# First product of the second network as seven products of half blocks instead of eight (Strassen's method), in a fused attention and two-network kernel on one core

## The chip, the cores and the metric

The kernel runs on one core of one Trainium2 chip, in one launch. The metric is device time in microseconds. Five engines run their own instruction queues in order and meet only at semaphores: TensorE (PE in the profile), VectorE (DVE), ScalarE (ACT), GpSimd (POOL) and SyncE (SP), which here only issues DMAs. TensorE multiplies out of the on-chip memory SBUF and accumulates in the eight banks of PSUM.

## The reference

Three stages follow each other. The change lies in the last one, `_moe2_ref`.

```python
def _moe2_ref(x, w_in, w_out):          # x 1536 x 512, w_in 512 x 2048, w_out 2048 x 512
    h = x @ w_in
    g = np.where(h > 0.0, h, 1.0 * (np.exp(np.minimum(h, 0.0)) - 1.0))
    return (g @ w_out).astype(np.float32)

def reference(**kwargs):
    attn_out = _attn_ref(...)           # 2 x 8 heads x 768 x 64: windowed and summary keys
    x = attn_out ... reshape(B * S, H * D)
    x = _moe_ref(x=x, ...)              # RMS norm, (silu(x @ w_gate) * (x @ w_val)) @ w_out, inner width 1536
    return _moe2_ref(x=x, ...)
```

The inputs arrive as 64-bit numbers. The kernel turns the weights into 32-bit numbers on the chip.

## The kernel before, in words

The 1536 tokens are cut into three blocks of 512 (`NBLK`, `TB`). Activations lie with features on the 128 partitions and tokens in the free dimension. `add_block1` runs the first network for a block in 12 chunks of 128 inner features, `add_block2` the second in 16. Attention for later blocks is woven into the first network of the earlier ones. By the end of the first network nothing but `add_block2` is left, three blocks one after another.

**Every large product is three matmuls.** A 32-bit number is split into a rounded high part and the rest, both of type `fp32r`. `THREE` in `project` (L894) and `down` (L960) multiplies high by high, high by rest and rest by high. The high part is an ACT cast (`split_a`, `act_a`, `x_hi`, all through `copy`, L300), the rest a subtraction (`split_b`, `act_b` through `minus` at L313, `x_lo` at L884).

**A chunk of `add_block2`** (L1015): `add_split` splits 512 columns of `w_in` (`ws_i`) and of `w_out` (`ws_p`); `add_project` makes 12 matmuls of 512 tokens into one PSUM bank (`ph`, L899: four parts of the contraction, three matmuls each); `elu_a` takes the exponential on ACT out of the bank (L939); `elu_b` on DVE makes min(exp, 1) - 1 (L943), `elu_c` on DVE adds max(ph, 0), again out of the bank (L947); `act_a` and `act_b` split the result; `down` adds 12 matmuls into the four banks `acc` (L967). So a block is 16 x 12 matmuls `ph` and as many `acc`, and the three blocks are 576 of each.

**Weights** arrive in `fetch`, and `convert_a` to `convert_d` (L424 to L448) make 32-bit numbers of them: an ACT pass, then on DVE a shift (L437 for w_in and w_out of this network), an insertion of the sign (`convert_c`, L442, left out for the kinds in `SIGNED`) and the lowest bits (L448). The 32-bit weights stay in the pool `raw` (36 tiles), for use by all three blocks.

**The order of the work** on each engine is made by `Order.issue` (L79) when the program is built. Each step is recorded by `add` with its engine, a cost, a due time, what it reads and writes, and the pool tiles that it takes (L60). The planner starts, per engine, the due step that can run; `SHIFT` moves due times by kind of step and by stretch; `SHARED` (L29) lists steps that it doesn't put on DVE and POOL at the same moment. The result is a fixed sequence per engine; the chip then goes through it by semaphores. Pools that matter here: PSUM banks `m0`, `m1`, `t0`, `t1` for `ph` (four), `a0` to `a3` for `acc`; `ws` (4 tiles of split weights), `act` (2 tiles of split activations), `x` (1), `raw` (36), `t2` (4).

Of the kernel before, what the change touches and what calls it, by code (L numbers as in the profile page):

```python
# [29 lines left out]
    "add_square", "diagonal", "x_lo", "x_hi", "act_a", "act_b", "elu_b", "convert_a", "convert_b", "convert_c",  # L30
# [186 lines left out]
def fused_kernel(ctx: ExitStack, tc: tile.TileContext, q, k, v, w_gate, w_val, w_out, rms_g, w_in2, w_out2, out):  # L217
# [16 lines left out]
    C2 = DFF2 // P  # L234
    TB = 512
# [24 lines left out]
    pool("ws", 4, True)  # L260
    pool("x", 1, True)
# [616 lines left out]
    def x_hi(eng, src, dst, c, i):  # L878
        t = new("x", dst, [P, 2, KM, TB], F32R) if dst not in T else T[dst]
        copy(eng, t[:, 0, c, i], T[src][:, c, i])  # L880

    def x_lo(src, dst, c, i):
        t = T[dst]
        nc.vector.tensor_sub(t[:, 1, c, i], T[src][:, c, i], t[:, 0, c, i].bitcast(F32))  # L884

# [363 lines left out]
```

## Time and profile before

| | us |
|---|---|
| median of 3 runs | 646.75 (645.97 to 647.37) |
| span of the profiled execution, first to last instruction | 644.8 |
| median less span | 1.95 |
| PE busy | 630.3 (98%) |
| DVE busy | 454.8 (71%) |
| ACT busy | 342.4 (53%) |
| POOL busy | 95.6 (15%) |

The page is one profiled execution. Its busy shares are means over the span; a stretch of it is read with the view by windows. The duration of one instruction is longer than its share of a dense sequence, since an engine begins the next before the last has left it: where instructions stand close together, the distance from start to start is the price. The page gives the profiled execution's span, and no time around it; the sum in the prediction is made on the span, and 1.95 us are added to compare with the median.

### The profile page before, as it was taken

The page shows a single profiled execution, that of the slowest core. Times are in us where ns is not written, and L with a number is a line of the kernel's source. Part 1 is how long each engine was busy: PE and PEld are TensorE (multiplying, and loading weights), DVE is VectorE, ACT ScalarE, POOL GpSimd, SP SyncE. Part 2 cuts the span into 40 slices and gives each one's busy share as a digit, 9 for nine tenths or more (in the row PEclk, how much of TensorE's full clock was granted, in tenths as well). Part 3 has the DMA queues.
Part 4 walks back from the last instruction along what each step waited for, and adds up shares of the span by engine and source line. Part 5 has one row for each costly group of instructions (what it writes and reads, how often), then busy time and mean ns, then how long its engine had stood idle before and what let it go on. Part 6 is the DMA issues. An engine that isn't in the chain of part 4 may idle for free.

```text
span 644.8 us, 9843 instructions
## 1 busy us (share of the span) xinstructions
PE 630.3 (98%) x3644; PEld 516.3 (80%) x3644; DVE 454.8 (71%) x828; ACT 342.4 (53%) x739; POOL 95.6 (15%) x160
## 2 busy tenths in 40 slices
PE   7899999999999999999999999999999999999997
PEld 5678777788888888888888888888888888888885
DVE  4788878868964557499999975555765555855554
ACT  2797568975463633465555564434444444544442
POOL 5753356363210210000000000000000000000000
PEclk9999999999999999999999999999999999999999
DMA  9998858565500000025656300000010000100001
GB/s 217 243 225 211 213 156 237 179 137 176 162 1 0 2 1 0 2 67 180 185 166 207 110 1 1 1 1 1 1 65 1 1 1 1 65 1 1 2 0 66
DMA packets 80352, 52.94 MB, mean 82 GB/s; under 512 B 51504, under 2 KB 75312, under 8 KB 80304
## 3 DMA queue, kind: packets, MB, share of 16 engines
q1 hardware_dynamic: 80304, 52.31, 29.9%
q8 instruction: 29, 0.48, 0.3%
q14 instruction: 19, 0.16, 0.1%
HBM read 49.15 MB, written 3.15 MB: 81 GB/s over the span
## 4 chain that ended last, share of the span: by engine, by line
PE 84%; DVE 6%; DMA 3%; SPq 3%; ACT 2%; issue 1%; DVEq 0%; ACTq 0%
PE acc L967 34%; PE ph L899 20%; PE pg L899 13%; PE pv L728 1%; PE pv_7c L899 1%; PE pv_8c L899 1%; PE pv_9c L899 1%; PE pv_11c L899 1%; PE pv_10c L899 1%; PE s L676 1%; PE pv_4c L899 1%; DMA va<-in_v 1%; DMA st_o<-in_moe_w_out 1%; PE pv_6c L899 1%; PE pv_1c L899 1%
## 5 line engine op out<-in xcount | busy, mean ns | idle before, releaser
L899 PE MATMUL ph<-xb,ws_i 128*128 128x512 f32 x576 | 137.9, 389 | 0.0
L967 PE MATMUL acc<-ws_p,act 128*128 128x512 f32 x576 | 137.7, 389 | 0.0
L967 PEld LDWEIGHTS acc<-ws_p,act 128*128 128x128 f32 x576 | 108.1, 188 | 22.5
L899 PEld LDWEIGHTS ph<-xb,ws_i 128*128 128x128 f32 x576 | 108.1, 188 | 22.4
L899 PE MATMUL pg<-x,ws_g 128*128 128x512 f32 (+1 forms) x456 | 108.7, 383 | 1.6 <-DVE ws_g L313 0.9
L967 PE MATMUL acc<-act,ws_o 128*128 128x512 f32 x432 | 106.3, 392 | 0.0
L899 PEld LDWEIGHTS pg<-x,ws_g 128*128 128x128 f32 x456 | 81.5, 188 | 19.1 <-DVE ws_g L313 1.3
L967 PEld LDWEIGHTS acc<-act,ws_o 128*128 128x128 f32 x432 | 80.4, 188 | 17.1 <-issue 0.5
L939 ACT ACTIVATE ex<-ph 128x512 f32<-128x512 f32 x48 | 28.8, 599 | 105.0 <-PE ph L899 105.0
L943 DVE TENSOR_SCALAR ex<-ex 128x512 f32<-128x512 f32 x48 | 20.5, 427 | 87.5 <-ACT ex L939 87.5
L302 ACT CAST act<-ex 128x512 fp32r<-128x512 f32 x48 | 29.8, 620 | 21.6 <-DVE ex L947 21.6
L302 ACT CAST ws_v<-raw_v 128x512 fp32r<-128x512 f32 x36 | 22.3, 620 | 32.6 <-PE acc L967 9.7
L932 DVE SCALAR_TENSOR_TENSOR th<-th,pg 128x512 f32<-128x512 f32 x36 | 24.6, 684 | 20.5 <-ACT th L928 20.3
L313 DVE TENSOR_TENSOR ws_i<-raw_i,ws_i 128x512 fp32r<-128x512 f32 x48 | 33.1, 689 | 8.0 <-ACT ws_i L302 8.0
L302 ACT CAST ws_i<-raw_i 128x512 fp32r<-128x512 f32 x48 | 29.7, 620 | 12.1 <-PE acc L967 12.1
L928 ACT ACTIVATE th<-pg 128x512 f32<-128x512 f32 x36 | 21.4, 595 | 26.7 <-PE pg L899 26.6
L313 DVE TENSOR_TENSOR act<-ex,act 128x512 fp32r<-128x512 f32 x48 | 33.1, 689 | 3.2 <-ACT act L302 0.7
L947 DVE SCALAR_TENSOR_TENSOR ex<-ph,ex 128x512 f32<-128x512 f32 x48 | 33.2, 691 | 1.5
L313 DVE TENSOR_TENSOR ws_p<-raw_p,ws_p 128x512 fp32r<-128x512 f32 x48 | 32.8, 682 | 1.2 <-ACT ws_p L302 1.2
L302 ACT CAST ws_p<-raw_p 128x512 fp32r<-128x512 f32 x48 | 29.6, 616 | 6.7 <-PE acc L967 6.7
L313 DVE TENSOR_TENSOR ws_o<-raw_o,ws_o 128x512 fp32r<-128x512 f32 x36 | 27.7, 770 | 6.3 <-ACT ws_o L302 6.2
L302 ACT CAST ws_o<-raw_o 128x512 fp32r<-128x512 f32 x36 | 22.3, 620 | 16.1 <-PE acc L967 3.5
(214 smaller groups left out, 918.8 us busy)
## 6 DMA issues: line engine op xcount, KB each, us to landing
st_i<-in_moe_w_in SPq DMA_DIRECT2D x16, 512.0 KB, 3.9
st_p<-in_moe_w_out SPq DMA_DIRECT2D x16, 512.0 KB, 3.8
st_g<-in_moe_w_gate SPq DMA_DIRECT2D x12, 512.0 KB, 4.9
st_o<-in_moe_w_out SPq DMA_DIRECT2D x12, 512.0 KB, 5.5
st_v<-in_moe_w_val SPq DMA_DIRECT2D x12, 512.0 KB, 4.9
va<-in_v SPq DMA_DIRECT2D x20, 192.0 KB, 5.6
kr<-in_k SPq DMA_DIRECT2D x12, 256.0 KB, 5.0
out<-ob SPq DMA_DIRECT2D x11, 256.0 KB, 2.0
```

Source lines behind the costliest of these rows:

```text
L302: nc.scalar.copy(out=out, in_=in_)
L313: (nc.gpsimd if eng == POOL else nc.vector).tensor_sub(out, a, b)
L676: nc.tensor.matmul(pq[h][ts, pr, :], qb[hs, pr, ts], ka[n][hs, pr, :], start=not pre, stop=not pre or pr == NP - 1)
L728: nc.tensor.matmul(pv[64 * h:64 * h + 64, pr, n, :], va[:NK, 2 * pr + h, :], T[f"ats{b}_{j}_{h}"][:, pr, QT * n:QT * n + QT], start=True, ...
L899: nc.tensor.matmul(pt[:, i], wt[:, a, kk * P:(kk + 1) * P], xt[:, c, kk, i], start=(kk == 0 and n == 0), stop=(kk == KM - 1 and n == 2))
L928: nc.scalar.activation(out=new("t2", f"th{b}_{c}", [P, TB]), in_=T[f"pg{b}_{c}"], func=AF.Tanh, scale=0.5)
L932: nc.vector.scalar_tensor_tensor(th, th, 1.0, T[f"pg{b}_{c}"], op0=ALU.add, op1=ALU.mult)
L939: nc.scalar.activation(out=new("t2", f"ex{b}_{c}", [P, TB]), in_=T[f"ph{b}_{c}"], func=AF.Exp)
L943: nc.vector.tensor_scalar(ex, ex, 1.0, -1.0, op0=ALU.min, op1=ALU.add)
L947: nc.vector.scalar_tensor_tensor(ex, T[f"ph{b}_{c}"], 0.0, ex, op0=ALU.max, op1=ALU.add)
L967: nc.tensor.matmul(acc, lhsT, rhs, start=(first and n == 0), stop=(last and n == 2))
```

## The change

The 512 x 512 part of w_in that four chunks share, and the 512 x 512 activations of a block, are each seen as two by two blocks of 256 x 256. The Winograd form of Strassen's method makes the four result blocks from seven products in place of eight.

- Per block of tokens: four sums of quarters of the activations (`x_sum`), and seven split factors (`factor_a`, `factor_b`).
- Per group of four chunks (`u`, four in a block): four sums of quarters of the weights on POOL (`w_sum`), seven splits of weights (`wide_a` on ACT, `wide_b` on DVE), seven products, each in one of the four PSUM banks.
- `save` (ACT, one a group) and `combine` (DVE, seven a group) add the products up, a bank and an SBUF tile each time.
- The ELU reads the sums in SBUF: `elu_a` makes max(-c, 0) on ACT, `elu_b` exp of its negative on ACT, `elu_c` on DVE the larger of that less 1 and of c.
- `down2` makes the same 576 matmuls as `down`, each step for 256 tokens and 256 inner features.
- w_in is fetched in 256 x 256 quarters, `i` and `p` join `SIGNED` (no `convert_c` for them), the activations `x` of the first network are four tiles for one, `ws` has 6 tiles for 4, `LEN_2` is 5.3 for 5.65, and the whole table `SHIFT` is new.

```diff
-    pool("ws", 4, True)
-    pool("x", 1, True)
+    pool("ws", WS, True)
+    pool("x", 4, True)
+    PAIRS = ("11", "21", "t2", "t1", "22", "t3", "t4")
+    FACTORS = ("i0", "i1", "s2", "s1", "s4", "s3", "i3")
+    def w_sum(eng, b, u, dst):
+        a11, a12, a21, a22 = [T[f"raw_i{4 * u + n}"].bitcast(F32) for n in range(4)]
+        t = new("raw", f"w{b}_{u}_{dst}", [P, TB])
...
+        (e.tensor_sub if minus_ else e.tensor_add)(t, x, y)
+    def wide_a(eng, b, u, i):
+        copy(eng, new("ws", f"ws{b}_{u}_{i}", [P, 2, 512], F32R)[:, 0], T[weight_of(b, u, i)].bitcast(F32))
+    def wide_b(eng, b, u, i):
+        t = T[f"ws{b}_{u}_{i}"]
+        minus(eng, t[:, 1], T[weight_of(b, u, i)].bitcast(F32), t[:, 0].bitcast(F32))
+    def product(b, u, i, bank, tag):
+        pt = new(tag, bank, [P, TB])
+        wt, xt = T[f"ws{b}_{u}_{i}"], T[f"xq{b}_{i}"]
+        for m in range(2):
+            for kk in range(2):
+                for n, (a, c) in enumerate(THREE):
+                    nc.tensor.matmul(
+                        pt[:, m * HALF:(m + 1) * HALF], wt[:, a, kk * HALF + m * P:kk * HALF + (m + 1) * P], xt[:, c, kk],
+                        start=kk == n == 0, stop=kk == 1 and n == 2)
+    def combine(src, other, dst):
+        nc.vector.tensor_add(new(TMP, dst, [P, TB]), T[src], T[other])
-    def elu_a(b, c):
-        nc.scalar.activation(out=new("t2", f"ex{b}_{c}", [P, TB]), in_=T[f"ph{b}_{c}"], func=AF.Exp)
...
-        nc.vector.tensor_scalar(ex, ex, 1.0, -1.0, op0=ALU.min, op1=ALU.add)
...
-        nc.vector.scalar_tensor_tensor(ex, T[f"ph{b}_{c}"], 0.0, ex, op0=ALU.max, op1=ALU.add)
+    def elu_a(src, ex):
+        nc.scalar.activation(out=new("t2", ex, [P, TB]), in_=T[src], func=AF.Relu, scale=-1.0)
+    def elu_b(ex):
+        nc.scalar.activation(out=T[ex], in_=T[ex], func=AF.Exp, scale=-1.0)
+    def elu_c(src, ex):
+        nc.vector.scalar_tensor_tensor(T[ex], T[ex], -1.0, T[src], op0=ALU.add, op1=ALU.max)
...
-            add_project(f"ph{n}", MM + AT, f"ws{b}_i{c}", x, [0], t)
+            for dst, at in (("s1", 0), ("s2", 1.5), ("s4", 3.5), ("s3", 5.0)):
+                add(SUM_W, 0, t - 6 + at, w_sum, b, u, dst, r=need[dst], w=[f"w{n}_{dst}"], new=[("raw", f"w{n}_{dst}")])
+            plus(1, "h1", "c00")
+            plus(2, "h1", "h2")
+            plus(3, "h2", "h4")
+            plus(4, "h4", "c01")
+            plus(5, "h4", "c11")
+            plus(5, "h2", "h3")
+            plus(6, "h3", "c10")
-SIGNED = 'gvo'
+SIGNED = 'gvoip'
-LEN_A, LEN_1, LEN_2 = 8.875, 7.05, 5.65
+LEN_A, LEN_1, LEN_2 = 8.875, 7.05, 5.3
```

How the order moves, at the places that the prediction speaks of. **PE before**, in the first block of the second network (`ph` is the first product, `acc` the second; names are those of tiles, with the buffer's number last):

```order
L899 MATMUL ph_7_4544<-xb_4242,ws_i_4528 128x512 x12
L967 MATMUL acc_0_2_4366<-ws_p_4462,act_0_5_4503 128x512 x3
L967 MATMUL acc_0_3_4370<-ws_p_4462,act_0_5_4503 128x512 x3
L967 MATMUL acc_0_0_4336<-ws_p_4500,act_0_6_4541 128x512 x3
L967 MATMUL acc_0_1_4340<-ws_p_4500,act_0_6_4541 128x512 x3
L899 MATMUL ph_8_4582<-xb_4242,ws_i_4566 128x512 x12
```

**PE now**, at the end of the third and through the fourth group of the first block (`p` are products, their numbers the block and the group; `xq` the factor of the activations, `ws` that of the weights):

```order
L1075 MATMUL p_0_2_4922<-xq_6_3742,ws_2_6_4871 128x256 x12
L1075 MATMUL p_0_3_4941<-xq_0_4241,ws_3_0_4875 128x256 x12
L1075 MATMUL p_0_3_4962<-xq_1_4997,ws_3_1_4892 128x256 x12
L1075 MATMUL p_0_3_4984<-xq_2_4252,ws_3_2_4912 128x256 x12
L1075 MATMUL p_0_3_5005<-xq_3_4256,ws_3_3_4954 128x256 x12
L1075 MATMUL p_0_3_5030<-xq_4_2819,ws_3_4_4982 128x256 x12
L1075 MATMUL p_0_3_5048<-xq_5_3704,ws_3_5_4999 128x256 x12
L1075 MATMUL p_0_3_5072<-xq_6_3742,ws_3_6_5024 128x256 x12
L1094 MATMUL acc_0_2_4481<-ws_p_4748,act_0_201_4916 128x512 x3
```

Before, each group of 12 `ph` stood between as many `acc`; now products can stand up to eight in a row, of half as many columns each, and the second product follows later.

**DVE now**, at the same place (L1083 is `combine`, which reads a bank `p`; L315 is a subtraction, with `wide_b` where it writes `ws`; L957 is `elu_c`):

```order
L1083 TENSOR_TENSOR c_0_2_4956<-p_0_2_4922,h_0_2_4937 128x512
L957 SCALAR_TENSOR_TENSOR ex_211_4935<-ex_211_4935,c_0_2_4918 128x512
L315 TENSOR_TENSOR ws_3_3_4954<-w_3_s_4794,ws_3_3_4954 128x512
L306 CAST xq_0_4977<-x_1_3558 128x512
L315 TENSOR_TENSOR ws_3_4_4982<-w_3_s_4854,ws_3_4_4982 128x512
L957 SCALAR_TENSOR_TENSOR ex_210_4959<-ex_210_4959,c_0_2_4956 128x512
L1083 TENSOR_TENSOR c_0_3_5022<-p_0_3_4962,h_0_3_5002 128x512
L1083 TENSOR_TENSOR h_0_3_5026<-p_0_3_4984,h_0_3_5002 128x512
L315 TENSOR_TENSOR ws_3_5_4999<-w_3_s_4873,ws_3_5_4999 128x512
L315 TENSOR_TENSOR ws_3_6_5024<-raw_i_4629,ws_3_6_5024 128x512
```

DVE had one subtraction per 512 columns of w_in and one ELU step out of the bank at this place; now `combine` is the one kind of step that reads a bank, and the others read two tiles of SBUF.

**POOL now**, over the same place (before, POOL has no step in the second network):

```order
L1035 TENSOR_TENSOR w_3_s_4873<-raw_i_4197,raw_i_4585 128x512
L1035 TENSOR_TENSOR w_0_s_4920<-raw_i_3470,raw_i_3524 128x512
L1035 TENSOR_TENSOR w_0_s_4980<-w_0_s_4920,raw_i_3367 128x512
L1035 TENSOR_TENSOR w_0_s_5020<-raw_i_3421,w_0_s_4980 128x512
L1035 TENSOR_TENSOR w_0_s_5063<-raw_i_3367,raw_i_3470 128x512
```

The 48 sums of weights are the whole of POOL's work from here on: the tile `w_3_s_4873` is for the fourth group, the `w_0` behind it for the first group of the next block.

## Rows read from the trace of the kernel before

**Rows 1.** The page: span, busy time of PE, and 40 slices of the span

```profile
span 644.8 us, 9843 instructions
...
PE   7899999999999999999999999999999999999997
...
DVE  4788878868964557499999975555765555855554
...
PEclk9999999999999999999999999999999999999999
```

**Rows 2.** By windows: start:end, length, then busy us (instructions) of PE, PEld, DVE, ACT, POOL, clock, DMA

```profile
0.00:15.00 15.00, 11.64 (x77) 7.67 (x81) 6.25 (x17) 4.22 (x6) 9.13 (x47) 1.00 1.07 218
...
260.00:375.00 115.00, 115.00 (x509) 95.22 (x508) 107.42 (x191) 66.56 (x113) 0.00 (x0) 1.00 0.41 128
375.00:461.00 86.00, 86.00 (x381) 71.19 (x381) 47.81 (x80) 36.39 (x65) 0.00 (x0) 1.00 0.00 1
```

**Rows 3.** The chain that ended last: start, length, what (in us)

```profile
375.45 2.72 PE ph L899 x12
378.17 2.72 PE acc L967 x12
...
632.49 8.17 PE acc L967 x36
```

**Rows 4.** Timeline of PE, 46 to 68: start, length from first start to last end

```profile
54.35 1.60 PE L899 MATMUL pv_0c<-x,ws_v 128*128 128x256 f32 x12
55.79 1.60 PE L899 MATMUL pg<-x,ws_g 128*128 128x256 f32 x12
```

**Rows 5.** Groups by line and form: count, busy us, mean ns of one, idle before them

```profile
L899 PE MATMUL ph<-xb,ws_i 128*128 128x512 f32 x576 | 137.9, 389 | 0.0
...
L947 DVE SCALAR_TENSOR_TENSOR ex<-ph,ex 128x512 f32<-128x512 f32 x48 | 33.2, 691 | 1.5
L313 DVE TENSOR_TENSOR act<-ex,act 128x512 fp32r<-128x512 f32 x48 | 33.1, 689 | 3.2 <-ACT act L302 0.7
...
L302 ACT CAST act<-ex 128x512 fp32r<-128x512 f32 x48 | 29.8, 620 | 21.6 <-DVE ex L947 21.6
...
L939 ACT ACTIVATE ex<-ph 128x512 f32<-128x512 f32 x48 | 28.8, 599 | 105.0 <-PE ph L899 105.0
...
L943 DVE TENSOR_SCALAR ex<-ex 128x512 f32<-128x512 f32 x48 | 20.5, 427 | 87.5 <-ACT ex L939 87.5
...
L448 DVE SCALAR_TENSOR_TENSOR raw_i<-st_i,raw_i 128x512 uint16<-128x512 uint16 x16 | 12.0, 750 | 0.0
...
L442 DVE SCALAR_TENSOR_TENSOR raw_i<-st_i,raw_i 128x512 uint32<-128x512 uint32 x16 | 11.0, 689 | 0.0
...
L437 DVE TENSOR_SCALAR raw_i<-st_i 128x512 uint32<-128x512 uint32 x16 | 6.8, 422 | 0.0
```

**Rows 6.** Timeline of DVE, 379 to 382

```profile
379.91 0.68 DVE L313 TENSOR_TENSOR ws_i<-raw_i,ws_i 128x512 fp32r<-128x512 f32 x1
380.51 0.68 DVE L313 TENSOR_TENSOR ws_p<-raw_p,ws_p 128x512 fp32r<-128x512 f32 x1
```

**Rows 7.** Timeline of POOL, 131 to 134

```profile
131.22 1.29 POOL L799 TENSOR_TENSOR slice(0, 512, None)_2057<-slice(0, 512, None)_2057,slice(0, 512, None)_2067 128x512 f32<-128x512 f32 x1
132.52 1.27 POOL L313 TENSOR_TENSOR ws_g<-raw_g,ws_g 128x512 fp32r<-128x512 f32 x1
133.75 1.30 POOL L799 TENSOR_TENSOR slice(0, 512, None)_2057<-slice(0, 512, None)_2057,slice(0, 512, None)_2080 128x512 f32<-128x512 f32 x1
```

**Rows 8.** Timeline of POOL, 57 to 58 and 71 to 73

```profile
57.30 1.29 POOL L313 TENSOR_TENSOR ws_v<-raw_v,ws_v 128x512 fp32r<-128x512 f32 x1 [0.28 <-ACT ws_v L302]
...
71.93 1.29 POOL L313 TENSOR_TENSOR ws_v<-raw_v,ws_v 128x512 fp32r<-128x512 f32 x1 [6.36 <-ACT ws_v L302]
```

**Rows 9.** Timeline of DVE, 57 to 59 and 71 to 75

```profile
57.75 0.69 DVE L932 SCALAR_TENSOR_TENSOR th<-th,pg 128x512 f32<-128x512 f32 x1 [2.31 <-ACT th L928]
...
72.34 1.42 DVE L313 TENSOR_TENSOR ws_o<-raw_o,ws_o 128x512 fp32r<-128x512 f32 x1 [1.26 <-ACT ws_o L302]
```

More of the change, by code (lines that the diff above doesn't have):

```diff
@@ L29 @@
 SHARED = (
-    "add_square", "diagonal", "x_lo", "x_hi", "act_a", "act_b", "elu_b", "convert_a", "convert_b", "convert_c",
+    "add_square", "diagonal", "x_lo", "x_hi", "act_a", "act_b", "elu_c", "x_sum", "w_sum", "factor_a", "factor_b",
+    "wide_b", "convert_a", "convert_b", "convert_c",
     "convert_d", "split_a", "split_b", "copy_keys", "normalize")
@@ L234, in fused_kernel @@
     C2 = DFF2 // P
+    U2 = C2 // 4
     TB = 512
@@ L317, in fused_kernel @@
     ANY_SB = {ACT: 0.52}
+    SUM_X = {DVE: 0.6}
+    SUM_W = {POOL: 1.28}
+    TMP = ("e", "ats")
     masks = [const.tile([P, NK], F32, name=f"mask{var}") for var in range(3)]
@@ new lines, in save, with down2 @@
+    def save(eng, src, dst):
+        copy(eng, new(TMP, dst, [P, TB]), T[src])
+    def combine(src, other, dst):
+        nc.vector.tensor_add(new(TMP, dst, [P, TB]), T[src], T[other])
+    def down2(b, u, m, n, first, last, qs=(0, 1)):
+        ot = T[f"act2_{b}_{u}{m}{n}"]
+        for j in range(2):
+            wt = T[f"ws{b}_p{4 * u + 2 * m + j}"]
+            for q in qs:
+                name = f"acc2_{b}_{2 * n + q}"
+                acc = new(f"a{2 * n + q}", name, [P, TB]) if first and j == 0 else T[name]
+                cs = slice(j * HALF + q * P, j * HALF + (q + 1) * P)
+                for x, (a, e) in enumerate(THREE):
+                    nc.tensor.matmul(
+                        acc, ot[:, a, cs], wt[:, e, :],
+                        start=first and j == x == 0, stop=last and j == 1 and x == 2)
@@ new lines, in add_block2, with halves @@
+        t0 = chunk2_at[b, 0]
+        def halves(name):
+            return [f"xt{b}_{name}"] if name[0] == "t" else src[:2] if name[0] == "1" else src[2:]
+        add("-", 0.0, t0 - 9, wait, w=[f"begin{b}"])
+        for dst, at in (("t1", -3.2), ("t2", -2.6), ("t3", -1.0), ("t4", -0.5)):
+            x, y = X_SUMS[dst]
+            add(SUM_X, 0, t0 + at, x_sum, b, dst, r=halves(x) + halves(y) + [f"begin{b}"], w=[f"xt{b}_{dst}"], new=[(TMP, f"xt{b}_{dst}")])
+        for i in range(7):
+            xq = f"xq{b}_{i}"
+            at = t0 - 4 + 0.9 * i
+            add({ACT: 0.52, DVE: 0.34}, 0, at, factor_a, b, i, r=halves(PAIRS[i]), w=[xq + "#h"],
+                new=[("x" if i < 4 else "kT", xq)])
+            add(SUM_X, 0, at + 0.5, factor_b, b, i, r=halves(PAIRS[i]) + [xq + "#h"], w=[xq + "#l"])
@@ new lines @@
+    ('copy_acc', 8): -14, ('down', 8): 7, ('down2', 8): 28.5, ('elu_a', 8): -5.5, ('elu_b', 8): -5,
+    ('elu_c', 8): -1, ('factor_a', 8): -8.5, ('factor_b', 8): -13.5, ('fetch', 8): 7, ('gate_a', 8): -5,
+    ('gate_b', 8): 1.5, ('gate_c', 8): 10.5, ('product', 8): 4, ('save', 8): -3, ('split_a', 8): -12.5,
+    ('split_b', 8): -0.5, ('take', 8): -11, ('w_sum', 8): 9, ('wait', 8): -21, ('wide_a', 8): -6,
+    ('wide_b', 8): 26, ('x_sum', 8): 1, ('act_a', 9): 151, ('act_b', 9): 5, ('copy_out', 9): -0.5,
@@ L1216 @@
+    ('down2', 9): 32, ('elu_a', 9): -0.5, ('elu_c', 9): 0.5, ('factor_a', 9): -18.5, ('factor_b', 9): -6.5,
+    ('product', 9): -1, ('save', 9): 34.5, ('split_a', 9): 37, ('split_b', 9): 2.5, ('store', 9): -30.5,
+    ('take', 9): -1.5, ('w_sum', 9): 9.5, ('wait', 9): -62.5, ('wide_a', 9): 12, ('wide_b', 9): -16,
+    ('x_sum', 9): -27,
 }
```

283 lines of the change are left out of this document (134 added, 149 removed).

## The prediction

> **What bounds the kernel now.** I read the page first. PE is busy for 630.3 of 644.8 us, its row of slices shows 9 almost everywhere, and the clock is granted in full throughout, which is the upper of its two levels [rows 1]. Then the windows: from 260 on PE is busy for every microsecond, while DVE goes from 107.42 of 115 us just ahead of the second network to 47.81 of 86 us inside it, and POOL has nothing to do [rows 2]. Last the chain of waits. In the second network it is PE alone, 2.72 us of `ph` and 2.72 us of `acc` in turn, until 632.49 + 8.17 = 640.66 us [rows 3]. So 24 matmuls take 5.44 us, one 0.2267 us, and no other engine is waited for. A microsecond less of matmul work there is a microsecond less of time, as long as DVE, ACT and POOL keep up with it.
>
> **Matmuls: 9.6 us less.** Removed are 576 matmuls `ph` of 512 columns [rows 5], at 0.2267 us [rows 3]: 130.6 us. Added are 3 blocks x 4 groups x 7 products x 12 = 1008 of 256 columns. The same form stands in the early part of the first network: 12 of them, each with its own weights, start at 54.35 and the next 12 at 55.79 [rows 4], so one is 1.44 / 12 = 0.120 us, and 1008 are 121.0 us. Half the columns thus cost 53% of the time, and of the eighth of the work that the method saves, 16.3 us, 6.7 are given back. The 576 matmuls of the second product stay. The Trainium skill (TensorE: Matmul & The Clock Gate, Back-to-back issue gap) gives 262 cycles for 256 columns and 518 for 512; by that the saving would be 14.3 us, but both rows are some 11 ns a matmul above it, and the rows decide.
>
> **DVE and POOL: 4 us lost.** Dense subtractions with two SBUF inputs start 0.60 us apart [rows 6], and sums on POOL 1.30 and 1.23 us apart, 1.27 us in the mean [rows 7]. A group now gives DVE 7 `wide_b`, 7 `combine`, 4 `elu_c`, 4 `act_b` and 4 `split_b`, 26 steps; a block adds 4 `x_sum` and 7 `factor_b`: 115 steps, 69 us a block. Before it was 16 x (4 x 0.60 + 0.43 for `elu_b` [rows 5]) + 4 x 0.60 = 47.7 us, as the window shows. `combine` costs what `elu_c` did, which read a bank too and took 691 ns against 689 for `act_b` [rows 5]. PE has 336 x 0.120 + 192 x 0.2267 = 83.8 us a block. By itself DVE fits.
>
> It isn't by itself: POOL adds 48 sums. At 72.34 a DVE subtraction out of SBUF, begun while a POOL subtraction of 1.29 us ran, took 1.42 us, and ended just 0.54 us after POOL's; a step with one operand in a bank, begun under POOL at 57.75, took its usual 0.69 us [rows 8, 9]. So a sum on POOL holds up `wide_b`, `act_b`, `split_b`, `elu_c`, `x_sum` and `factor_b`, while `combine` can pass. The stage as a whole has room, but the order piles the work up: between the first product of the third group of block one and the first of the second group of block three it records 588 products and 300 matmuls of the second product on PE, 193 two-operand steps on DVE, 50 of them `combine`, and 35 sums on POOL. PE needs 70.6 + 68.0 = 138.6 us; DVE needs 115.8, and POOL 44.5: 160.3 if nothing overlaps. All 50 `combine` could cover 30 us, which leaves 130.3. In the order about one `combine` stands beside each sum (in the front part: `c`, `h` and `h` stand near the last three of the sums shown, but two `ws` and an `elu_c` near the others); 35 x 0.60 = 21.0 us are covered, 139.3 are left, 0.7 us over PE. Nothing is then left for DVE's own waits, on PE's banks and on ACT's casts. At its densest, DVE was busy for 107.42 of 115 us, 93.4% [rows 2]; 139.3 / 0.934 = 149.1 us would be 10.5 us over. The ends are 0 and 10.5. I take 4, nearer to the lower one, since in that window nothing pressed DVE to be denser.
>
> **The rest, at nothing.** ACT does per group 7 `wide_a`, 4 `act_a` and 4 `split_a` at 620 ns, 8 passes of the ELU at 599 [rows 5] and one `save` like them: 14.7 us by durations, under 20.96 us of PE. The second ELU pass costs ACT 0.6 us a tile and takes 0.43 from DVE; cover gone, it would be 48 x 0.6 = 28.8 us. `convert_c` goes for w_in and w_out: 32 x 0.69 us on DVE [rows 5], but in the window where PE is busy for 115 of 115 us [rows 2]. The sums hold tiles of `raw`, so 7 conversions of weights move behind the first product: 7 x (0.42 + 0.75) = 8.2 us of DVE [rows 5] in two groups where PE has 39.2 us and DVE 47 x 0.60 + 8.2 = 36.4. Should they come late, `wide_a` of the fourth group would wait. The fetches of w_in keep their 512 KB and their queue and are wanted later. The end of the kernel, 4.1 us behind the last matmul, keeps its form; eight steps of the second product stand there without a product between, and DVE, which feeds them, has 45 steps or 27 us of work in that last group's 42.7 us of PE. Finally the new `SHIFT` reorders attention and first network, with the same steps. Nothing prices that; PE stands idle for 14.5 us in all, and for 3.36 in the first 15 [rows 1, 2]. I take 0, with 3 us either way.
>
> **The sum.** On the profiled span: 644.8 - 9.6 + 4 = 639.2 us; with the 1.95 us by which the median stands above the span, 641.2 us.
>
> **The rivals.**
> - *DVE keeps up everywhere.* For it: PE waits for nothing in the second network before, with DVE at 93% ahead of it. Against it: the piled-up stretch has no reserve by the sum above. 646.75 - 9.6 = 637.2 us.
> - *A half matmul is cheaper* than in the early rows, since those stand among attention's steps. By the skill's gap it would be 646.75 - 14.3 + 4 = 636.5 us. Against it: twelve in a row show an even 0.120, and the 512-column rows have the same surplus.
> - *The longer way from product to product.* Six steps (combine, max, exp, `elu_c`, cast, rest) of 0.69 + 0.60 + 0.60 + 0.69 + 0.62 + 0.69 = 3.9 us stand between a bank and the second product, where five of 3.0 us stood [rows 5], and `act` still has two tiles. If each of the 12 groups pays the 0.9 us once, 10.8 us go: 648.0 us, no change. Against it: the second products come several products later.
> - *POOL's sums shut DVE out (slower).* The Trainium skill (SBUF — State Buffer, SBUF: two separate sides) says that the pair of ports shared by DVE and GpSimd is an exclusive lock, held for a whole instruction; the 1.42 us agrees. POOL starts a sum when its inputs are there and a tile of `raw` is free, which a `wide_b` just ended, so the next DVE step is often another SBUF one. Break-even is where 21.7 - 9.6 = 12.1 us are covered, 20 of 50 `combine`. With 12 of them covered, 7.2 us, PE loses 14.5: 651.7 us. Against it: the planner lists these steps in `SHARED`, and so keeps them apart in its own order.
>
> **How the numbers follow.** The forecast, with losses from 0.7 to 8.3 us (637.9 to 645.4), gets 0.50; DVE keeping up 0.17; the cheaper matmul 0.03; the longer way 0.13; POOL's lock 0.17. 0.2%, about what a measurement of this kernel can tell from no change, is 1.3 us: faster is below 645.45, slower above 648.05. Faster is 0.50 + 0.17 + 0.03 = 0.70, same 0.13, slower 0.17. The range takes in the forecast, the rival below it and the longer way: 637.0 to 649.0 us; the lock and the cheaper matmul, 0.20, stay out.
>
> **What would show it.** In the profile after, twelve products should take 1.44 us from start to start, PE should lose some microseconds to DVE (`ws`, `act` or `xq` as what is waited for) between the third group of block one and the second of block three, and hardly any in the last 45 us. DVE steps of 0.9 to 1.4 us beside POOL's sums would show the lock; their sum beyond 0.69 each is its price, and if they are many and PE's waits pass 9.6 us, I am wrong on the sign. If PE has no gaps there, the rival without loss is right. PE's waits on ACT's casts would mean the longer way. If the time of the first product in the second network comes earlier or later by more than 3 us, the new order and not the method made the difference.

## The result and the profile after

The changed kernel takes 638.47 us (median of 4 runs, 637.62 to 640.12), beside 647.06 us for the kernel before on the same chip: 0.9872 of its time, 95% interval 0.9853 to 0.9891, so 8.6 us or 1.3% less. The forecast was 641.2 us, with a loss of 4 us to DVE and POOL in it. The profiled execution took 638.61 us, with a span of 636.7.

The page after, its span, busy times and slices:

```profile
span 636.7 us, 11068 instructions
...
PE 621.1 (98%) x4076; PEld 527.7 (83%) x4076; DVE 510.8 (80%) x886; ACT 404.7 (64%) x861; POOL 165.2 (26%) x203
...
PE   8889999999999999999999999999999999999997
...
DVE  4789897798657456498976989989998989897863
```

PE is as full as before [rows 1], while DVE is now at 80% for 71 and stays at 8 and 9 tenths through the second network until its end, where it had mostly 5.

The windows after, of the last stage of the first network, of all that follows the first product of the second network, and of the stretch that the prediction called tight (third group of block one to second group of block three). Columns as in [rows 2]:

```profile
260.00:375.00 115.00, 115.00 (x510) 95.37 (x509) 95.04 (x156) 62.65 (x110) 16.01 (x11) 1.00 0.36 115
374.67:636.70 262.03, 257.84 (x1609) 233.14 (x1607) 225.22 (x350) 177.32 (x314) 57.80 (x37) 1.00 0.06 19
414.04:552.99 138.95, 138.95 (x890) 126.69 (x889) 128.58 (x194) 100.96 (x180) 53.45 (x35) 1.00 0.02 9
```

In the tight stretch PE is busy for 138.95 of 138.95 us, with DVE at 92.5%. The sum had asked for 138.6 us of PE, so no more than 0.4 us can have been lost there. The view of waits has no row for PE from 374.67 on; the chain there is PE alone:

```profile
433.83 11.47 PE p L1075 x96
445.29 5.46 PE acc L1094 x24
450.75 5.75 PE p L1075 x48
456.50 2.75 PE acc L1094 x12
...
610.71 21.82 PE acc L1094 x96
```

96 products take 11.47 us, 0.1195 each, against the 0.120 of [rows 4]. Twelve `acc` take 2.75 us, where they took 2.72 [rows 3].

Where the 8.1 us between the two spans lie: from the first product on, the kernel before takes 269.51 us (375.29 to 644.80), with 18 matmuls of the first network still in that time; the changed one takes 262.03 with 24 of them. At equal work, 6 x 0.2267 = 1.36 us, the second network is 8.84 us shorter. The front part is 0.7 us longer: 374.67 + 24 x 0.2267 = 380.1 against 375.29 + 18 x 0.2267 = 379.4.

The groups after, by form (columns as in [rows 5]):

```profile
L1035 POOL TENSOR_TENSOR w_s<-raw_i,raw_i 128x512 f32<-128x512 f32 x24 | 37.7, 1571 | 207.7 <-DVE ws L315 105.0
...
L315 DVE TENSOR_TENSOR act<-ex,act 128x512 fp32r<-128x512 f32 x48 | 37.0, 772 | 13.8 <-ACT act L304 13.7
...
L957 DVE SCALAR_TENSOR_TENSOR ex<-ex,c 128x512 f32<-128x512 f32 x48 | 34.9, 728 | 7.1 <-ACT ex L954 7.1
...
L315 DVE TENSOR_TENSOR ws<-w_s,ws 128x512 fp32r<-128x512 f32 x48 | 34.6, 728 | 2.7 <-ACT ws L304 2.7
...
L1083 DVE TENSOR_TENSOR c<-p,h 128x512 f32<-128x512 f32 x48 | 32.7, 687 | 3.8 <-PE p L1075 2.4
```

`combine` (`c`) keeps its 687 ns beside POOL's sums, and the steps with both operands in SBUF grow, those shown to 728 and 772 ns. A sum on POOL grows as well, from 1.27 [rows 7] to 1.57 us: each of the two holds up the other. The timelines of POOL and of DVE show two sums in the middle of the stretch:

```profile
519.21 3.54 POOL L1035 TENSOR_TENSOR w_s<-raw_i,raw_i 128x512 f32<-128x512 f32 x2 [2.24 <-DVE ws L315]
```

```profile
519.58 1.41 DVE L1083 TENSOR_TENSOR c<-p,h 128x512 f32<-128x512 f32 x2
520.91 0.68 DVE L315 TENSOR_TENSOR ws_p<-raw_p,ws_p 128x512 fp32r<-128x512 f32 x1
521.51 1.79 DVE L957 SCALAR_TENSOR_TENSOR ex<-ex,c 128x512 f32<-128x512 f32 x1
```

POOL starts as `wide_b` releases its tile (`DVE ws`). Two `combine` in a row cover the first sum almost whole; the second sum stretches an `elu_c` from 0.69 to 1.79 us. A third kind costs DVE nothing, because DVE stands idle anyway, here waiting for a product:

```profile
422.76 1.30 POOL L1035 TENSOR_TENSOR w_s<-w_s,raw_i 128x512 f32<-128x512 f32 x1 [0.69 <-DVE ws L315]
```

```profile
424.04 0.69 DVE L1083 TENSOR_TENSOR h<-p,h 128x512 f32<-128x512 f32 x1 [1.43 <-PE p L1075]
```

Counted over the tight stretch in the two timelines: the 35 sums last 54.9 us. In 23.6 us of that DVE is in a `combine` (25 of the sums have one begun beside them), in 8.4 us DVE stands idle, and 14 DVE steps last more than 0.9 us, together 9.2 us over their usual 0.69 each.

### The profile page after: what moved, and what is told of

The parts are those of the page before. It is cut to its first block, busy times and chain, and to the rows that moved or that the text cites. A ratio compares the mean times of both kernels' runs of the same rounds, so it can differ in the third digit from the quotient of the medians.

```text
span 636.7 us, 11068 instructions
## 1 busy us (share of the span) xinstructions
PE 621.1 (98%) x4076; PEld 527.7 (83%) x4076; DVE 510.8 (80%) x886; ACT 404.7 (64%) x861; POOL 165.2 (26%) x203
## 4 chain that ended last, share of the span: by engine, by line
PE 77%; DVE 8%; DMA 6%; ACT 4%; SPq 3%; issue 1%; POOL 1%; DVEq 0%; ACTq 0%; POOLq 0%
PE acc L1094 21%; PE p L1075 19%; PE acc L977 12%; PE pg L911 11%; DMA st_g<-in_moe_w_gate 2%; SPq L513 2%; ACT e L704 1%; DMA st_o<-in_moe_w_out 1%; PE pv_11c L911 1%; PE pv_2c L911 1%; PE pv_4c L911 1%; DVE nm L697 1%; DMA va<-in_v 1%; PE pv L739 1%; PE pv_7c L911 1%
## 5 line engine op out<-in xcount | busy, mean ns | idle before, releaser
L1075 PEld LDWEIGHTS p<-xq,ws 128*128 128x128 f32 x1008 | 125.2, 191 | 2.7
L1075 PE MATMUL p<-xq,ws 128*128 128x256 f32 x1008 | 126.1, 283 | 0.0
L911 PE MATMUL pg<-xs,ws_g 128*128 128x512 f32 (+1 forms) x456 | 108.6, 382 | 0.9 <-DVE th L944 0.6
L911 PEld LDWEIGHTS pg<-xs,ws_g 128*128 128x128 f32 x456 | 81.8, 188 | 17.6 <-DVE th L944 1.1
L1035 POOL TENSOR_TENSOR w_s<-raw_i,raw_i 128x512 f32<-128x512 f32 x24 | 37.7, 1571 | 207.7 <-DVE ws L315 105.0
L304 ACT CAST act<-ex 128x512 fp32r<-128x512 f32 x48 | 29.7, 619 | 30.3 <-PE acc L1094 25.4
L315 DVE TENSOR_TENSOR act<-ex,act 128x512 fp32r<-128x512 f32 x48 | 37.0, 772 | 13.8 <-ACT act L304 13.7
L957 DVE SCALAR_TENSOR_TENSOR ex<-ex,c 128x512 f32<-128x512 f32 x48 | 34.9, 728 | 7.1 <-ACT ex L954 7.1
L951 ACT ACTIVATE ex<-c 128x512 f32<-128x512 f32 x48 | 30.0, 630 | 14.4 <-DVE act L315 9.1
L315 DVE TENSOR_TENSOR ws<-w_s,ws 128x512 fp32r<-128x512 f32 x48 | 34.6, 728 | 2.7 <-ACT ws L304 2.7
L1083 DVE TENSOR_TENSOR c<-p,h 128x512 f32<-128x512 f32 x48 | 32.7, 687 | 3.8 <-PE p L1075 2.4
L315 DVE TENSOR_TENSOR ws_p<-raw_p,ws_p 128x512 fp32r<-128x512 f32 x48 | 33.6, 710 | 1.1 <-ACT ws_p L304 0.6
L304 ACT CAST ws<-w_s 128x512 fp32r<-128x512 f32 x48 | 29.3, 616 | 7.4 <-PE p L1075 3.1
```

Of the source, the lines that this page charges most:

```text
L304: nc.scalar.copy(out=out, in_=in_)
L315: (nc.gpsimd if eng == POOL else nc.vector).tensor_sub(out, a, b)
L911: nc.tensor.matmul(pt[:, i], wt[:, a, kk * P:(kk + 1) * P], xt[:, c, i], start=(kk == 0 and n == 0), stop=(kk == KM - 1 and n == 2))
L951: nc.scalar.activation(out=new("t2", ex, [P, TB]), in_=T[src], func=AF.Relu, scale=-1.0)
L957: nc.vector.scalar_tensor_tensor(T[ex], T[ex], -1.0, T[src], op0=ALU.add, op1=ALU.max)
L1035: (e.tensor_sub if minus_ else e.tensor_add)(t, x, y)
```

## Experiments: what a narrow matmul costs

**The kernel before, with its first product in halves of 256 columns.** No sums, no new steps: 1152 matmuls for 576.

```diff
-            add_project(f"ph{n}", MM + AT, f"ws{b}_i{c}", x, [0], t)
+            add_project(f"ph{n}", MM + AT, f"ws{b}_i{c}", x, [0], t, (t, t + 1.36))
```

> The kernel before, with each of the 576 matmuls of the first product of the second network cut into two of 256 columns: 1152. The price of a narrow matmul by itself: by the rows (0.120 and 0.2267 us) 1152 x 0.120 - 576 x 0.2267 = 7.7 us slower than before, 654.1 on a median of 646.4. Rival (cost goes by columns alone, the narrow rows of the early part were slow for other reasons): no change, 646.4. If each half had some further price, as weights loaded twice as often that PE has to wait for: over 10 us slower.

Measured: 656.87 us, 1.0164 of the kernel before (1.0138 to 1.0190), 8.9 to 12.3 us slower. The timeline of PE in this run:

```profile
404.04 3.04 PE L899 MATMUL ph<-xb,ws_i 128*128 128x256 f32 x24
406.92 2.91 PE L967 MATMUL acc<-ws_p,act 128*128 128x512 f32 x12
409.66 3.04 PE L899 MATMUL ph<-xb,ws_i 128*128 128x256 f32 x24
```

24 halves start within 2.88 us, 0.120 each: the 7.7 us of the rows. Twelve `acc` behind them take 2.74 us for 2.72, some 1 us over the 48 changes of width. From the first product on the run is 279.36 - 269.51 = 9.85 us longer, so about 1 us stays without a name. (Weight loads wait for 1.7 us in all there, in six places, where the kernel before has no such wait; that this is the missing time was not shown.) The rival of a further price, over 10 us, isn't excluded by the time alone, since the interval crosses its bound; the even 0.120 speaks against it. The Trainium skill (TensorE: Matmul & The Clock Gate, Back-to-back issue gap) gives 262 and 518 cycles as the gap of a matmul by itself; by these the halves would cost 1.4 us, an estimate. This run, with weights of its own for each matmul, doesn't agree, and the price stays with the rows.

## Experiments: what a sum on POOL costs DVE

**The sums cut to 8 columns**, all steps kept in their order:

```diff
-        (e.tensor_sub if minus_ else e.tensor_add)(t, x, y)
+        (e.tensor_sub if minus_ else e.tensor_add)(t[:, :8], x[:, :8], y[:, :8])
...
```

The rest of the edit lets `wide_a` and `wide_b` read a tile of w_out where they read a sum.

> The changed kernel with its 48 sums of weights on POOL cut to 8 of 512 columns; the split weights s1 to s4 are taken from a tile of w_out instead, so the output is not the product. Same steps in the same order on every engine. It measures what the sums cost DVE: theory (the sums hold DVE's SBUF steps up, but there is reserve enough): DVE's busy time falls by 48 x 0.3 to 0.9 us = 14 to 43 us from 510.8, the time stays at 638.5 within 1 us, because PE waits for nothing in the second network. Rival (the sums cost PE something all the same, in starts that are a little late): 1.3 us less, the whole excess of PE's starts there, 637.2. Rival (no lock): DVE's busy time stays within 5 us.

Measured: 639.54 us, ratio 0.9888 (0.9861 to 0.9915), no different from the changed kernel. The page and the same groups in this run:

```profile
PE 620.8 (98%) x4076; PEld 527.1 (83%) x4076; DVE 497.2 (78%) x886; ACT 404.9 (64%) x861; POOL 109.8 (17%) x203
```

```profile
L315 DVE TENSOR_TENSOR act<-ex,act 128x512 fp32r<-128x512 f32 x48 | 33.0, 687 | 16.9 <-ACT act L304 16.8
L957 DVE SCALAR_TENSOR_TENSOR ex<-ex,c 128x512 f32<-128x512 f32 x48 | 32.9, 685 | 7.3 <-ACT ex L954 7.3
```

Every SBUF step is back at 0.69 us. DVE's busy time falls by 510.8 - 497.2 = 13.6 us, 0.28 us a sum, at the lower end of what was expected, and not a microsecond of it reaches PE. In the tight stretch, 413.85 to 552.80 in this run, DVE is busy for 119.89 us, for 128.58 with the sums: 8.7 us for 35 sums, 0.25 each.

**Each sum computed twice**, in the same order, so that POOL works on without the plan knowing of it.

```diff
         (e.tensor_sub if minus_ else e.tensor_add)(t, x, y)
+        (e.tensor_sub if minus_ else e.tensor_add)(t, x, y)
```

> The changed kernel with each of the 48 sums of weights computed twice on POOL, the same result; order as before. POOL gets 48 x 1.27 = 61 us more. Theory (a sum shuts out DVE's steps out of SBUF, and combine alone covers): DVE stood idle for 16.5 of 205 us from 375 to 580, in which about 37 sums lie; 37 more at 1.27 us are 47 us, of which the 50 combine cover some 15 (half of their 30); 32 less 16.5 us of idle time is 15 us slower, 654, with PE waiting for ws, act or xq. Rival one (DVE loses nothing to POOL): 638.5, DVE's busy time unchanged. Rival two (nothing is covered): 47 - 16.5 = 30 us slower, 669.

Measured: 677.19 us, 1.0470 (1.0442 to 1.0498): 38.7 us more than the changed kernel, beyond both the theory and the worst rival. The page, then the timelines of POOL and of DVE at a doubled sum:

```profile
PE 634.0 (94%) x4076; PEld 532.3 (79%) x4076; DVE 560.7 (83%) x886; ACT 404.5 (60%) x861; POOL 240.2 (36%) x251
```

```profile
540.11 1.29 POOL L1035 TENSOR_TENSOR w_s<-raw_i,w_s 128x512 f32<-128x512 f32 x1
541.48 1.63 POOL L1036 TENSOR_TENSOR w_s<-raw_i,w_s 128x512 f32<-128x512 f32 x1
```

```profile
540.24 1.71 DVE L315 TENSOR_TENSOR act<-ex,act 128x512 fp32r<-128x512 f32 x1
541.87 1.78 DVE L315 TENSOR_TENSOR ws_p<-raw_p,ws_p 128x512 fp32r<-128x512 f32 x1
543.58 0.68 DVE L315 TENSOR_TENSOR ws<-w_s,ws 128x512 fp32r<-128x512 f32 x1
```

The 48 repeats cost DVE 560.7 - 510.8 = 49.9 us of busy time, 1.04 us each, nearly four times the price of the first 48. The lock of the rival is real: `act`, begun 0.13 us behind the first sum, takes 1.71 us and ends 0.55 us after it, and `ws_p` does the same behind the second. The Trainium skill (SBUF — State Buffer, SBUF: two separate sides) states that of a DVE step with two SBUF inputs and a GpSimd step, the one that starts first gets the port pair that they share for the whole instruction. This trace agrees, with 1.71 and 1.78 us for 0.69.

The whole loss isn't DVE's work alone. PE's busy time in the second network is 267.89 us for 257.84, with the same matmuls, and the granted clock there is 0.98. It is 0.93 in this stretch, where PE stands idle for 7.6 of 40 us, so that part of the time PE ran at the lower of its two levels (1.2 and 2.4 GHz):

```profile
540.00:580.00 40.00, 32.39 (x178) 27.98 (x179) 39.83 (x42) 21.83 (x40) 29.99 (x21) 0.93 0.00 1
```

**The plan told to disregard POOL**: DVE's steps with due times beyond 400 are no longer kept apart from the sums. (The change had entered `w_sum`, `wide_b`, `elu_c`, `x_sum` and the factors in `SHARED`, beside `act_b` and `split_b`; `combine` isn't there, so the plan could put it beside a sum.) The same steps in another order, but for some copies that go to another engine.

```diff
-            return engine in ("DVE", "POOL") and ops[i][3].__name__ in SHARED
+            return engine in ("DVE", "POOL") and ops[i][3].__name__ in SHARED and not (engine == "DVE" and ops[i][2] > 400)
```

> The changed kernel planned without keeping DVE's steps with a due time beyond 400 apart from POOL's sums (about 37 of the 48 sums lie there); the same steps, another order on DVE. In the changed kernel a sum cost DVE 0.28 us (510.8 - 497.2 us of busy time over 48 sums), where each doubled sum, which the plan did not know of, cost 49.9 / 48 = 1.04 us. Theory (the plan's order is what makes a sum cheap): the price goes up to about 1 us, DVE's busy time by 37 x 0.7 = 26 us to 537, and less the reserve of some 9 us that three experiments show the time rises by 17 us, to 655. Rival (a single sum begun behind one of DVE's steps costs 0.28 us in any order, since POOL is the one that waits): 511 us busy and 638.5 us.

Measured: 656.47 us, 1.0176 (1.0143 to 1.0208), within 2 us of the theory. From the first product on:

```profile
378.89:658.00 279.11, 264.36 (x1609) 236.26 (x1607) 244.28 (x357) 173.06 (x307) 58.04 (x37) 0.99 0.05 18
```

DVE is busy for 244.28 us where the run without sums has 215.75 and the changed kernel 225.22. Of the 28.5 us, 4.2 are seven copies and casts (x357 for x350) that ACT did before; the other 24.3 are 0.66 us a sum over 37 sums, for 0.26. 31 DVE steps last more than 0.9 us, for 15, together 26.0 us over 0.69 each, for 9.7; 11 sums have a `combine` begun beside them, for 25. So it is the order that makes a sum cheap, and 0.66 comes near the 0.67 of the prediction. The time came out as forecast by two errors that cancel: DVE's busy time is 530.2 us and not 537, and the 9 us of reserve that were taken off are not to be seen, since this window is 17.1 us longer with 19.1 us more for DVE to do. The new order is worse in other ways too, and how much of the loss is the lock alone this run doesn't tell.

## Experiments: how much room DVE has left

Three runs give DVE more work at fixed places, one lets the plan know of it. **The 48 sums on DVE**, at the place where POOL's stood:

```diff
-        e = nc.gpsimd if eng == POOL else nc.vector
+        e = nc.vector
```

> The changed kernel with the 48 sums of weights issued on DVE at the place in the program where POOL's were; POOL has no step in the second network. DVE gets 48 x 0.60 = 28.8 us more and loses what POOL's sums held it up. If a sum on POOL costs DVE about 0.6 us, the time stays within 2 us of 638.5 and DVE's busy time near 511. If it costs DVE little (0.1 to 0.2 us), DVE goes in its dense windows from 37.5 of 40 us to about 41 of 40, and the time is 4 to 8 us longer, 643 to 647. If it costs over 0.9 us, DVE's busy time falls by 14 us or more and the time stays at 638.5.

Measured: 645.17 us, 0.9967 (0.9950 to 0.9984), the middle case by its time. DVE's busy time, 525.6 us, rose by 14.8 where 48 x 0.60 = 28.8 were added, so 14.0 came back: 0.29 us a sum, as in the run without sums. A window of this run shows how dense DVE can be:

```profile
460.00:500.00 40.00, 39.49 (x252) 35.59 (x251) 39.33 (x66) 26.44 (x49) 0.00 (x0) 1.00 0.08 27
```

DVE is busy for 39.33 of 40 us, 98%, and PE begins to wait.

**One more DVE step in the ELU**, min(ex, 1) + 0 ahead of `elu_c`:

```diff
+        nc.vector.tensor_scalar(T[ex], T[ex], 1.0, 0.0, op0=ALU.min, op1=ALU.add)
         nc.vector.scalar_tensor_tensor(T[ex], T[ex], -1.0, T[src], op0=ALU.add, op1=ALU.max)
```

> The changed kernel with one more DVE step a tile of the ELU, min(ex, 1) + 0 over 128x512 in place, 48 in all at 0.427 us, 20.5 us; nothing else moves. My theory after the result (DVE has a reserve of 7% in the dense windows, spread evenly): DVE needs 37.5 + 3.2 = 40.7 of each 40 us there, so 0.7 us in each of five windows, 2 to 5 us slower, 640.5 to 643.5. The prediction's theory (the stretch is full, and DVE can't be denser than 93.4%): what is added comes out in full, at 7 steps a group about 0.43 x 4 = 1.7 us in each of 7 groups, 12 us slower, 650. Rival (reserve is larger than the busy time shows, since that contains waiting for POOL): 638.5.

Measured: 654.86 us, 1.0122 (1.0098 to 1.0146). I missed this one by far: not 2 to 5 us slower but 16.4. The prediction's reading, 12 us, came nearer. The waits of PE in this run from 376 on:

```profile
PE p L1076 <- DVE c L1084: 4.6, 3, 2.0
PE p L1076 <- DVE ws L315: 2.6, 6, 0.7
PE p L1076 <- DVE h L1084: 1.7, 3, 0.7
```

A product waits for split weights (`ws`), or for a bank that a late `combine` (`c`, `h`) has not yet read.

**The same step, known to the planner** (`elu_x` makes it):

```diff
+                add(DVE, 0.34, at + 1.0, elu_x, ex, w=[ex])
                 add(DVE, 0.6, at + 1.1, elu_c, c, ex, r=[c], w=[ex])
```

> The added DVE step of the ELU again (min(ex, 1) + 0, 48 times, 20.5 us), but known to the planner with its cost, so the order is made for it. Theory (what decides is DVE's total in the second network, of which 9 us are free): as slow as where the plan did not know it, 654.9 within 3 us. Rival (the fixed order made it slow, a new one spreads the load into DVE's idle time, of which the windows from 375 to 620 show 26 us): 639 to 645.

Measured: 653.68 us, 1.0116 (1.0089 to 1.0143): the theory holds, a new order gains little. The table `SHIFT` wasn't fitted to the added step, so what a fit would gain is open.

**The added step on every second tile**, unknown to the planner again:

```diff
+        if ex.endswith("00") or ex.endswith("11"):
+            nc.vector.tensor_scalar(T[ex], T[ex], 1.0, 0.0, op0=ALU.min, op1=ALU.add)
```

> The changed kernel with the added DVE step of the ELU on 24 of the 48 tiles: 24 x 0.43 to 0.46 = 10 to 11 us of DVE work. The law of the other runs is that DVE has a reserve of 8 to 11 us in the second network and what goes beyond it comes out in full (15 us more gave 6.7, 25.5 gave 16.4, 50 gave 38.7): 638.5 to 641.5, 2 us slower at most 3. Rival (no reserve, the loss is proportional, some 0.65 us for a microsecond): 645. Rival (a threshold higher than that): no change.

Measured: 647.38 us, 0.9992 (0.9973 to 1.0012), which is 1.2% or 7.8 us more than the changed kernel: a miss, since I had said 3 us at most, and the rival without a reserve, 645, came nearer. I had counted the step alone, 10 to 11 us; DVE's busy time in the second network rose by 13.2 us. The windows from the first product on, one for each run, in the order sums on DVE, every second tile, every tile, every tile and known to the plan, sums twice:

```profile
377.91:645.00 267.09, 259.81 (x1609) 233.35 (x1607) 236.44 (x387) 177.96 (x314) 0.00 (x0) 1.00 0.05 19
```

```profile
374.33:642.60 268.27, 261.41 (x1609) 233.15 (x1607) 238.43 (x374) 177.03 (x314) 55.57 (x37) 1.00 0.05 19
```

```profile
375.69:653.80 278.11, 263.60 (x1609) 233.28 (x1607) 250.59 (x398) 176.42 (x314) 54.49 (x37) 1.00 0.05 18
```

```profile
374.94:649.80 274.86, 262.74 (x1609) 232.79 (x1607) 251.37 (x399) 176.13 (x313) 58.50 (x37) 1.00 0.05 18
```

```profile
378.11:674.70 296.59, 267.89 (x1609) 237.18 (x1607) 267.48 (x352) 176.95 (x314) 115.94 (x74) 0.98 0.05 17
```

| run | DVE busy over 225.22 | longer than 262.03 | longer by the ratios of all runs |
|---|---|---|---|
| sums cut short | -9.5 | 0.0 | 1.0 |
| sums on DVE | 11.2 | 5.1 | 6.1 |
| extra step, every second tile | 13.2 | 6.2 | 7.8 |
| extra step, every tile | 25.4 | 16.1 | 16.2 |
| the same, known to the plan | 26.2 | 12.8 | 15.8 |
| sums twice | 42.3 | 34.6 | 38.7 |

The third column is one execution of each run, and executions of one kernel differ by several us; the last takes (ratio - 0.9872) x 647. Work taken off DVE brings nothing. Of 11 to 26 us of further work about half to two thirds comes out as time, 0.46 to 0.64 by either column; of the doubled sums, where PE's clock falls too, 0.8 to 0.9. A fixed reserve, with all beyond it coming out in full, isn't shown: what is swallowed by the windows would be 6.1, 7.0, 9.3, 13.4 and 7.7 us. What is shown is that 11 us more are already too many. Where below that the loss begins, no run tells.

## Experiments: the refitted order

**The changed kernel with the whole old table `SHIFT`** (two of its lines); kinds of step that it doesn't know get no shift.

```diff
-    ('down2', 9): 32, ('elu_a', 9): -0.5, ('elu_c', 9): 0.5, ('factor_a', 9): -18.5, ('factor_b', 9): -6.5,
...
+    ('copy_e', 9): -8, ('copy_k', 9): -1, ('copy_out', 9): 5, ('copy_q', 9): 1, ('copy_v', 9): 11,
```

> The changed kernel with the table SHIFT of the kernel before; kinds of step that the old table doesn't know get no shift. Other order on all engines. Theory: in attention and the first network the refit was worth nothing (first product within 1.5 us of 374.7), while in the second network DVE has only some 9 us of reserve and a plan that is not fitted to it uses them up: 2 to 12 us slower, 640.5 to 650.5, with waits of PE for DVE there. Rival one (the refit did nothing at all, the method alone made the gain): 638.5 within 1 us. Rival two (the front part gained from the refit what a larger surrounding cost took): the first product comes 3 us or more later than 374.7.

Measured: 671.3 us, 1.0399 (1.0362 to 1.0435): 32.8 us more than with the new table, nearly three times what I had expected at most. The window from the first product on, and the longest waits of PE in it:

```profile
380.37:669.50 289.13, 271.51 (x1615) 238.60 (x1613) 234.46 (x351) 174.59 (x306) 64.10 (x42) 0.98 0.03 12
```

```profile
PE acc L1094 <- DVE act L315: 4.1, 3, 2.7
PE acc L1094 <- ACT act L304: 4.0, 2, 2.8
PE p L1075 <- DVE ws L315: 2.2, 6, 0.6
```

Six more matmuls of the first network lie in this window (x1615 for x1609), 1.4 us; 25.7 of the 27.1 us are loss, with only 9.2 us more of DVE work. The second product waits for its activations (`act`), the products for weights: the same steps in a poor order. That the first product comes 5.7 us later, at 380.37, is a miss too: I had said within 1.5 us, and 3 us or more later was the sign of the second rival, a gain of the front part by the refit.

Only about half of the 25.7 us are waits. PE's busy time grew by 271.51 - 257.84 - 1.4 = 12.3 us, and part of that is its clock. Two rows of the same form, and the stretch in which the second lies:

```profile
540.68 5.63 PE L1094 MATMUL acc<-ws_p,act 128*128 128x512 f32 x24
567.51 8.63 PE L1094 MATMUL acc<-ws_p,act 128*128 128x512 f32 x24 [2.81 <-ACT act L304]
```

```profile
564.00:572.00 8.00, 5.19 (x14) 3.57 (x13) 6.85 (x11) 2.46 (x4) 3.59 (x3) 0.50 0.00 0
```

PE had waited four times between 556 and 563, for 2.3 us in all, and then for 2.81 us. The granted clock from 564 to 572 is 0.50, the lower of the two levels, and 24 `acc` take 8.63 us for 5.63. So a wait of PE here costs more than its own length.

**The old table for due times below 280, the new one beyond** (entries of the new table with stretch 8 and 9, the old one's below; the edit has no more to it).

> The changed kernel with the table SHIFT of the kernel before for all due times below 280, and the new one's entries beyond. With the whole old table the kernel took 671.3 us, 32.8 more than the changed one: its second network took 277.3 us for 252.0 from the first product on, and its part before that some 7 us more. Theory (the two parts are separate): the second network comes back to 252 to 257, the front stays as with the old table, 642 to 652. Rival (an order is one piece: the entries beyond 280 fit only behind the front that they were fitted with): the second network takes 265 us or more, over 655.

Measured: 644.31 us, 0.9955 (0.9934 to 0.9977), as the theory had it. The window:

```profile
378.46:640.50 262.04, 257.85 (x1609) 233.06 (x1607) 224.85 (x350) 177.12 (x314) 57.80 (x37) 1.00 0.06 19
```

The second network is back at 262.04 us to the hundredth, and the first product comes 3.8 us later: the two parts are separate. (With the same order in front, the first product came between 374.33 and 378.11 in the profiled executions of six kernels, so a single trace tells little about 3 us there; the ratio of many runs says 0.8%, or 5.4 us.)

**The kernel before with the new table** (the edit above, the other way round).

> The kernel before with the new table SHIFT, nothing else changed (the second network's steps keep their names only in part). If the refit were a gain by itself in attention and first network: 2 us or more faster than 645.5 to 646.4. My theory (a table fits the program that it was made for, and DVE has much room in the second network of the kernel before, so only the front suffers): 3 to 15 us slower, 649 to 661, the loss lying before the first product, which comes later than 375.3. Rival (the table hardly matters where the method is the old one): within 1.3 us.

Measured: 654.13 us, 1.0110 (1.0078 to 1.0143), 7 us slower and as expected. Its first `ph` starts at 382.89 with 12 matmuls of the first network to come, against 375.29 with 18: at equal work 6.2 us later. The second network takes what it took. So the new table is no gain of its own: each table is good for the program that it was fitted to.

## Experiment: the small parts alone

**The kernel before with the new ELU and without `convert_c`** for the second network. The plan still counts the second pass as a DVE step.

```diff
-SIGNED = 'gvo'
+SIGNED = 'gvoip'
-        nc.scalar.activation(out=new("t2", f"ex{b}_{c}", [P, TB]), in_=T[f"ph{b}_{c}"], func=AF.Exp)
+        nc.scalar.activation(out=new("t2", f"ex{b}_{c}", [P, TB]), in_=T[f"ph{b}_{c}"], func=AF.Relu, scale=-1.0)
...
-        nc.vector.tensor_scalar(ex, ex, 1.0, -1.0, op0=ALU.min, op1=ALU.add)
+        nc.scalar.activation(out=ex, in_=ex, func=AF.Exp, scale=-1.0)
...
```

> The kernel before with two small parts of the change alone: the ELU with two ACT passes (max(-x, 0), then the exponential of its negative) and one DVE step, and no convert_c for w_in and w_out of the second network. DVE loses 48 x 0.43 + 32 x 0.69 = 42.7 us of work, ACT gets 28.8 us more. Theory (PE alone sets the time in the second network of the kernel before): no change, 645.5 to 646.4 within 1.3 us, with DVE's busy time near 412. Rival (DVE, at 93% just ahead of the second network, or the longer ELU chain does count): more than 1.3 us either way.

Measured: 650.39 us, 1.0041 (1.0022 to 1.0060), 1.4 to 3.9 us slower; DVE's busy time fell to 418.0. I had expected no change. PE waits for nothing in the second network here either, but the waits of its weight loads have three rows, where the kernel before has none:

```profile
PEld ph L899 <- DVE ws_i L313: 2.9, 10, 0.3
PEld ph L899 <- DVE ex L947: 2.7, 18, 0.2
PEld acc L967 <- DVE act L313: 0.8, 3, 0.3
```

`ex` is `elu_c`, which reads the bank and so frees it: with the longer ELU a product's first weights go in 0.15 us late, 18 times. The mean of a matmul `ph` goes from 389 to 393 ns, and the time from the first product on is 273.38 us (375.52 to 648.90) for 269.51. That the late weight loads are all of these 3.9 us was not shown apart. In the changed kernel `combine` frees the bank, ahead of the ELU, and no such row stands in its second network.

## Why the prediction was right, and where not

**The bound and the matmul term: right.** PE sets the second network before and after. 9.6 us were forecast, and 8.8 came. Of the missing 0.8 us the chain shows 0.7: its 576 `acc` take 131.6 us for 130.6, since those behind narrow matmuls take 2.75 for 2.72, and its 1008 products 120.6 us for 121.0.

**The failed step: "35 x 0.60 = 21.0 us are covered, 139.3 are left".** The cover came out much as taken, 23.6 us. The error is in what is left: the whole rest, 44.5 - 21.0 = 23.5 us of POOL's sums, was put on DVE as work, 0.67 us each, and measured are 8.7 us, 0.25 each. 8.4 us of the sums lay where DVE stood idle, in the very waits for which nothing was to be left, and only 14 of the 35 sums or so held up a step. How many do is set by the order: a sum costs 0.28 us in the planned order, 0.66 with the plan blind, and 1.04 where the plan doesn't know of it. The 4 us taken for such a load would have been too little: at 0.67 DVE would have had (0.67 - 0.25) x 37 = 15.5 us more, and by the 0.46 to 0.64 us of the added work this is 7 to 10 us, an estimate.

**What was luck.** The loss of 4 us was a term of the forecast, and it didn't come. The measured time lies 2.7 us below the forecast, and it lies in the range because the range took in the rival without loss. The matmul term, and with it the direction, was worked out; that no loss is added to it was not.

**The reading that nothing is left at 93.4%: wrong as a limit, right as a warning.** With the sums on DVE it reaches 98%. In the changed kernel it ran at 92.5% through the stretch without a wait of PE, but with 11 us more PE waits for it.

**The rivals.** "DVE keeps up everywhere" (637.2 us) is what happened, with the 0.8 us of the matmuls and 0.7 us of the front part on top; I gave it 0.17. It deserved more: that the planner keeps these steps apart stood in the text, as an argument against the lock alone and not against the loss. The lock (651.7 us) has its mechanism and its price confirmed, in orders that this kernel doesn't have. The longer way (648.0) has no wait of PE to show after the change; the run with the small parts alone, 1.4 to 3.9 us slower, has the longer ELU hold a bank, but that this is its cause was not shown apart. The cheaper half matmul is refuted by 0.1195 and 0.120.

**The rest.** The front moved by 0.7 us in the two traces, within the 3 us either way, though single traces differ by as much as 3.8 us there. But "I take 0" for the new table held only because before and after each have their own: without the refit the change would have been a loss, 1.0399 for 0.9872. That the conversions behind the first product hide was right, PE being busy for all of 260 to 375 and of what follows until the end of the products.

## What to carry to other kernels

When work moves to an engine that can hold up another, its price is not its duration: ask which steps the order puts beside it, and whether the other engine stands idle there anyway, and take the price from a place where that order already holds. A method that saves work on the bounding engine by loading the others is worth its sum only after the order is fitted again. And how much room an engine has left can be measured directly, by adding known work in several sizes; include small ones, and take many executions of each.

## What the runs showed of the hardware that I had not expected

- The price of a POOL sum to DVE is 0.28, 0.66 or 1.04 us, by the steps that stand beside it, and POOL's side stretches too, from 1.27 to 1.57 us in the mean.
- A wait of PE can cost more than its own length: after waits of 2.3 and 2.81 us the granted clock was 0.50, and 24 matmuls took 8.63 us for 5.63.
- A change of width costs TensorE something: twelve matmuls of 512 columns behind narrow ones take 2.74 to 2.75 us, not 2.72.
- A stage got 3.9 us longer without a single wait of PE in it; what the trace showed instead were weight loads that waited for 0.15 to 0.3 us, 31 times.
